# Attention with a gated feed-forward block: gates as rows through DRAM, transposes by DMA, layer normalizing on ScalarE, and a new instruction order

## The chip, the cores and the metric

One core of one Trainium2 chip. The metric is the time on the device in microseconds (us), as the median of several executions; a kernel's executions mostly agree within a few tenths of a per cent (three of the four of the kernel before took 253.68 to 254.1 us). A run counts as slow when it lies over 1.5% above the fastest run of the same kernel, and only fast runs enter the ratios. TensorE (PE in the profile) multiplies matrices, PEld is its weight load, VectorE (DVE), ScalarE (ACT) and GpSimd (POOL) do the rest, and SyncE (SP) issues transfers (DMA). The program gives each engine its own list of instructions, in a fixed order; where an input is not there yet, the engine waits (in the changed kernel VectorE stood 3.89 us for one transfer, with two normalizings behind it that did not need it).

## The reference

```python
def reference(A_x, A_wqkv, A_wo, B_x, B_w1, B_w3, B_w2, c, w_mod):
    # sizes: x (1, 2048, 512), wqkv (512, 1536), w1, w3 (512, 1792), w2 (1792, 512), w_mod (512, 3072), bfloat16
    def _A_ref(x, wqkv, wo):
        H, W, dil = 32, 8, 2                  # 32 heads of 16; a query sees 8 keys, 2 apart
        # ... cut: q, k, v; gather of 8 keys and values per query; softmax over the 8
        return (...).reshape(B, S, D) @ wo
    def _B_ref(x, w1, w3, w2):
        return (_silu(x @ w1) * (x @ w3)) @ w2          # written with einsum
    x = A_x
    mod = (_silu(c) @ w_mod).reshape(c.shape[0], 6, 1, -1)
    # ... cut: sa, ca, ga, sb, cb, gb are the six rows of mod
    h = _layernorm(x, axis=-1) * (1 + ca) + sa          # LN1
    x = x + ga * _A_ref(h, A_wqkv, A_wo)                # first gate
    h = _layernorm(x, axis=-1) * (1 + cb) + sb          # LN2
    x = x + gb * _B_ref(h, B_w1, B_w3, B_w2)            # second gate
    return x
```

The 2048 rows are handled as 16 tiles of 128.

## The kernel before

The gates are not applied to the activations: the weights `wo` and `w2` are scaled by them once. For that a gate has to lie in all 128 partitions, which four products with a stationary matrix of equal columns (`csb`) give directly. The attention weights of a tile go to DRAM (`a_scratch_dram`) and come back in another layout (`sb_al`), because there the 8 window positions lie in partitions.

```python
# Every instruction is recorded with its cost in a small model; the model plays the engines
# and so fixes, once, the order of each engine's instructions.
    def dma(self, out, in_, key, nbytes, r=(), w=(), part=(), after=(), eng="sp", cost=450, group=None):
        nc = self.nc

        def fn(e):
            a = out() if callable(out) else out
            b = in_() if callable(in_) else in_
            with nc.allow_non_contiguous_dma(reason="layout"):
                return e.dma_start(a, b)

        o = self.op(eng, fn, cost, key, r=r, w=w, part=part, after=after, dma=nbytes)
        if group is not None:
            group.append(o)
            o.group = group
        return o

    def schedule(self, prio):
        # ... cut: picks, engine by engine, the ready operation of highest priority
                if o.dma:
                    dma_free = max(busy[e], dma_free) + o.bytes // DMA_RATE
                    o.end = dma_free + LAT["sp"]
                else:
                    o.end = busy[e] + LAT[e]
        # ... cut

    def gate(i):
        k = ("mod", 4 + i)
        vm = Val("ps_gate", psum)

        def mm(e):
            for t in range(KT):
                ins = e.matmul(bank(vm), csb[:, t, :], wm_g[i][:, t, :], start=(t == 0), stop=(t == KT - 1))
            return ins

        p.op("pe", mm, 4 * MM, k, r=[vwmg[i], vcsb] + wm_hold, w=[vm])
        dst = (ga_bc, gb_bc)[i]
        p.op("act", lambda e: e.activation(dst[:], bank(vm), ACT.Copy), c_act(512), k, r=[vm], w=[vg[i]])

    def ln_stats(which, T):
        i = which * NT + T
        k = ("st", i)
        vs, vm = Val("st"), Val("mv")
        o = p.op("dve", lambda e: e.bn_stats(st[:, i, :], x_sb[:, T, :]), 670, k, r=[vx[T]], w=[vs])
        p.op("dve", lambda e: e.bn_aggr(mv[:, i, :], st[:, i, :]), 190, k, r=[vs], w=[vm], lead=o)
        va, vr = Val("var"), Val("rstd")
        o = p.op("pool", lambda e: e.tensor_tensor(rs[:, i, :], mv[:, i, 1:2], cst[:, 0:1], ALU.add), 350, k, r=[vm, vcst],
                 w=[va])
        p.op("pool", lambda e: e.tensor_tensor(rs[:, i, :], rs[:, i, :], cst[:, 1:2], ALU.pow), 550, k, r=[va, vcst],
             w=[vr], lead=o)
        vn = Val("xn", xnpool)
        p.op("dve", lambda e: e.tensor_scalar(vn.at[:], x_sb[:, T, :], mv[:, i, 0:1], rs[:, i, :], op0=ALU.subtract,
                                              op1=ALU.mult), 350, ("nm", i), r=[vx[T], vr, vm], w=[vn])
        return vn

    def ln_T(which, gi, vns):
        # ... cut: for each tile 4 transposes on TensorE into PSUM (120 ns a pair in the model),
        # then per feature block one eviction that applies the modulation (ScalarE, or VectorE
        # for half of the first two LN1 groups)

    def values(T, i, ve, va):
        vad, val = Val("ad"), Val("al", alpool)
        p.dma(bass.AP(a_dram, T * P * W * H, [[W * H, 16], [16 * W * H, 8], [1, W * H]]),
              lambda: ve.at[0][:, i].rearrange("p w h -> p (w h)"), ("ad", T), 65536, r=[va, ve], w=[vad], cost=400)
        p.dma(lambda: val.at[:], bass.AP(a_dram, T * P * W * H, [[H, P], [16 * W * H, 8], [1, H]]), ("al", T), 65536 * 3,
              r=[vad], w=[val], cost=400)
        vv = Val("vsh", vshpool)
        loads = []
        for g in range(0, 8, VG):
            p.dma(lambda g=g: vv.at[:, g:g + VG, :].rearrange("p g d -> p (g d)"),
                  bass.AP(v_dram, (PAD + T * P + g) * D, [[8 * D, 16], [-DIL * D, W], [1, VG * D]]), ("vl", T), VG * 131072,
                  r=[vv_dram[T]] + ([vv_dram[T - 1]] if T else [vvpad]), part=[vv], group=loads)

        # ... cut: one VectorE product of 128x4096 elements (value rows times attention weights),
        # 32 small products that add up the window (TensorE), then the output projection, which
        # reads `wo` already scaled by the first gate

    # ... cut; the order in which the program is recorded:
    gate(0)
    p.op("dve", lambda e: e.tensor_tensor(wo[:], wo[:], bass.AP(ga_bc, 0, [[D, P], [0, KT], [1, D]]), ALU.mult), 1200,
         ("mod", 6), r=[vwo, vg[0]], w=[vsc_wo])
    modulation(1)
    gate(1)
    # ... cut: the same for w2 in two halves, then attention in 8 blocks, then 5 FFN groups
```

The softmax here doesn't subtract the row's maximum and nothing guards it: scores larger than these inputs give would overflow.

## Time and profile before

| | before |
|---|---|
| median of 3 runs | 254.03 us (253.68 to 254.1) |
| span of the profiled run | 253.2 us |
| TensorE busy | 239.0 us (94%) |
| VectorE busy | 191.7 us (76%), over 90% from 20 to 175 us |
| first large product | 10.51 us |

The lines behind this stand in the prediction.

### The profile page before, as it was taken

To read this page: it belongs to the slowest core of one execution; us is meant where nothing else is said; L and a number is where in the kernel's file an instruction comes from. 1 tells how busy PE (TensorE), PEld (TensorE's weight loads), DVE (VectorE), ACT (ScalarE), POOL (GpSimd) and SP (SyncE) were. 2 spreads that over 40 slices of the span, in tenths; PEclk is the share of its full clock that TensorE was granted. 3 is DMA by queue.
4 is the path that set the end of the run, shared out by engine and by line. 5 is a ranking of instruction groups with operands and counts; after the bars stand their busy time and mean duration, and the time that the engine had idled before them with its cause. 6 is when DMAs were issued, how large, how long until landed. Compare 5 with 4: busy or idle time off the path is not lost.

```text
span 253.2 us, 5473 instructions
## 1 busy us (share of the span) xinstructions
PE 239.0 (94%) x2262; PEld 140.4 (55%) x2296; DVE 191.7 (76%) x298; ACT 111.4 (44%) x198; POOL 32.0 (13%) x81
## 2 busy tenths in 40 slices
PE   0599989999999999999999999999999999999995
PEld 0367555655488666546654544556544444565562
DVE  4759889999998989999899899999952443432432
ACT  2159748864863347432462273334234322420120
POOL 6237641001000040000002200020030000000000
PEclk9999999999999999999999999999999999999999
DMA  6997999899954595322369145393001000000101
GB/s 193 359 324 189 293 350 331 210 331 284 241 123 140 142 310 196 64 31 62 106 194 295 54 104 85 87 310 103 4 0 44 0 0 21 21 3 21 41 23 41
DMA packets 45817, 36.29 MB, mean 143 GB/s; under 512 B 19408, under 2 KB 36576, under 8 KB 45792
## 3 DMA queue, kind: packets, MB, share of 16 engines
q1 hardware_dynamic: 45264, 35.94, 49.4%
q8 instruction: 18, 0.29, 0.5%
q10 hardware_dynamic: 528, 0.00, 0.1%
q14 instruction: 7, 0.06, 0.1%
HBM read 30.67 MB, written 5.26 MB: 142 GB/s over the span
## 4 chain that ended last, share of the span: by engine, by line
PE 87%; DVE 5%; DMA 2%; POOL 2%; issue 1%; SPq 0%; ACT 0%; DVEq 0%
PE pall L771 36%; PE pall L792 19%; PE pall L615 9%; PE pall L755 5%; PE pall L742 5%; PE pall L633 5%; PE pall L673 4%; PE pall L574 2%; DMA sb_x<-in_A_x_dram 2%; POOL sb_rs L555 1%; DVE sb_xn L558 1%; DVE sb_st L550 1%; POOL sb_rs L553 1%; DVE sb_pq L664 1%; DVE sb_hh L780 1%
## 5 line engine op out<-in xcount | busy, mean ns | idle before, releaser
L771 PE MATMUL pall<-sb_h,sb_w 128*128 128x512 bf16 (+1 forms) x548 | 100.0, 336 | 0.7
L771 PEld LDWEIGHTS pall<-sb_h,sb_w 128*128 128x128 bf16 x560 | 53.7, 97 | 41.4
L777 ACT ACTIVATE sb_sg<-pall 128x512 bf16<-128x512 f32 (+1 forms) x70 | 35.6, 511 | 70.6 <-PE pall L771 70.3
L780 DVE TENSOR_TENSOR sb_hh<-sb_sg,pall 128x512 bf16<-128x512 bf16 (+1 forms) x70 | 39.5, 577 | 26.0 <-PE pall L771 23.8
L792 PE MATMUL pall<-sb_w,sb_hh 128*128 128x512 bf16 x216 | 49.7, 379 | 0.4
L664 DVE TENSOR_TENSOR sb_pq<-sb_q,sb_kT 128x4096 bf16<-128x4096 bf16 x16 | 36.4, 2283 | 0.5 <-ACT sb_q L622 0.3
L792 PEld LDWEIGHTS pall<-sb_w,sb_hh 128*128 128x128 bf16 x224 | 21.4, 98 | 23.5 <-DVE sb_hh L780 0.2
L615 PE MATMUL pall<-sb_h,sb_wqkv 128*128 128x512 bf16 (+1 forms) x155 | 31.9, 344 | 0.3
L582 ACT ACTIVATE sb_h<-pall,sb_modc 128x512 bf16<-128x512 bf16 (+1 forms) x36 | 23.1, 708 | 18.7 <-PE pall L574 13.1
L553 POOL TENSOR_TENSOR sb_rs<-sb_mv,sb_cst 128x1 f32<-128x1 f32 x32 | 8.8, 276 | 151.4 <-DVE sb_mv L551 148.4
L733 DVE TENSOR_TENSOR sb_vsh<-sb_vsh,sb_al 128x4096 bf16<-128x4096 bf16 x12 | 27.3, 2285 | 0.4 <-DMA sb_vsh<-v_scratch_dram 0.4
L798 DVE TENSOR_TENSOR sb_o<-pall,sb_x 128x512 bf16<-128x512 f32 x16 | 11.0, 688 | 18.0 <-PE pall L792 18.0
L550 DVE BATCH_NORM_STATS2 sb_st<-sb_x 128x6 f32<-128x512 bf16 x32 | 21.8, 682 | 3.3 <-DMA sb_x<-in_A_x_dram 3.2
L555 POOL TENSOR_TENSOR sb_rs<-sb_rs,sb_cst 128x1 f32<-128x1 f32 x32 | 20.9, 654 | 2.5
L615 PEld LDWEIGHTS pall<-sb_h,sb_wqkv 128*128 128x128 bf16 x160 | 15.1, 101 | 11.0 <-ACT sb_h L582 0.7
L633 PE MATMUL pall<-sb_wqkv,sb_h 128*128 128x512 bf16 x63 | 17.6, 411 | 1.5 <-DVE sb_xn L558 1.3
L574 PE MATMUL pall<-sb_ident,sb_xn 128*128 128x128 bf16 x128 | 12.8, 227 | 6.4 <-DVE sb_xn L558 6.4
L673 PEld LDWEIGHTS pall<-sb_E,sb_pq 128*128 128x128 bf16 x512 | 14.7, 96 | 2.7 <-DVE sb_pq L664 0.6
L748 ACT ACTIVATE sb_ot<-pall 128x512 bf16<-128x512 f32 x16 | 9.6, 598 | 13.6 <-PE pall L742 13.6
L574 PEld LDWEIGHTS pall<-sb_ident,sb_xn 128*128 128x128 bf16 x128 | 9.5, 101 | 10.6 <-DVE sb_xn L558 6.9
L755 PE MATMUL pall<-sb_wo,sb_ot 128*128 128x512 bf16 x58 | 15.0, 379 | 0.3
L673 PE MATMUL pall<-sb_E,sb_pq 128*128 128x32 bf16 x512 | 15.1, 177 | 0.0
(59 smaller groups left out, 163.8 us busy)
## 6 DMA issues: line engine op xcount, KB each, us to landing
sb_vsh<-v_scratch_dram SPq DMA_DIRECT2D x48, 256.0 KB, 4.4
sb_vshx<-v_scratch_dram SPq DMA_DIRECT2D x16, 256.0 KB, 4.5
sb_wm_s<-in_w_mod_dram SPq DMA_DIRECT2D x2, 1024.0 KB, 6.6
v_scratch_dram<-sb_v SPq DMA_DIRECT2D x16, 128.0 KB, 5.0
sb_w<-in_B_w_dram SPq DMA_DIRECT2D x4, 512.0 KB, 7.9
out_dram<-sb_o SPq DMA_DIRECT2D x16, 128.0 KB, 1.7
sb_w<-in_B_w_dram SPq DMA_DIRECT2D x1, 1792.0 KB, 8.9
sb_wqkv<-in_A_wqkv_dram SPq DMA_DIRECT2D x3, 512.0 KB, 7.9
```

Of the source, the lines that this page charges most:

```text
L550: o = p.op("dve", lambda e: e.bn_stats(st[:, i, :], x_sb[:, T, :]), 670, k, r=[vx[T]], w=[vs])
L574: ins = e.transpose(b[:, col:col + P], vns[tt].at[:, ft * P:(ft + 1) * P], ident[:])
L615: ins = e.matmul(bank(vp)[:, 0:n], wqkv[:, t, col:col + P], vh.at[:, t, 0:n], start=(t == 0), stop=(t == KT - 1))
L633: ins = e.matmul(bank(vp), vh.at[:, t, tt * P:(tt + 1) * P], wqkv[:, t, 2 * D:3 * D], start=(t == 0), stop=(t == KT - 1))
L664: return e.tensor_tensor(vp.at[:], in0, in1, ALU.mult)
L673: ins = e.matmul(b[:, c0:c0 + H], vp.at[:, w, ft, :], E_sb[:, ft, :], start=(ft == 0), stop=(ft == KT - 1))
L733: return e.tensor_tensor(v_w, v_w, a_w, ALU.mult)
L755: ins = e.matmul(bank(vy), vt.at[:, ft, :], wo[:, ft, :], start=(ft == 0), stop=(ft == KT - 1))
L771: ins = e.matmul(bank(vp)[:, 0:n], wt[:, t, fi * P:(fi + 1) * P], vh.at[:, t, 0:n], start=(t == 0), stop=(t == KT - 1))
L777: p.op("act", lambda e: e.activation(vt.at[:, 0:n], bank(vgp)[:, 0:n], ACT.Silu), c_act(n), k, r=[vgp], w=[vt], table="silu")
L780: p.op("dve", lambda e: e.tensor_tensor(vh_.at[:, 0:n], vt.at[:, 0:n], bank(vup)[:, 0:n], ALU.mult), c_dve(n), k, r=[vt, vup], w=[vh_])
L792: ins = e.matmul(bank(vz), vhh[fi].at[:, tt * P:(tt + 1) * P], w2[:, fi, :], start=(fi == 0), stop=(fi == NF - 1))
```

## The change

Its intent: take work off TensorE and VectorE and close TensorE's gaps. (1) Idle products come before the first real ones, so that those no longer run at half pace (422 ns for 512 columns at 10.5 us in the kernel before, against 216 later). (2) `c` is loaded as four rows and transposed, the first loads are merged. (3) A gate is computed as columns, transposed to rows, written to DRAM and spread over the partitions by two GpSimd DMAs. (4) LN2 is normalized on ScalarE, with a bias made by two small GpSimd steps, and for FFN groups 1 to 4 transposed by DMA. (5) The attention weights' trip is issued by GpSimd. (6) The last two tiles are computed and stored in halves. A pair of LN1 evictions of the second group goes from VectorE to ScalarE. (7) All priorities, and so the order of every engine, are new; the scheduling model now also treats GpSimd's DMAs differently. The core of the diff (cut: sizes and aliases of buffers, the calls of (1), the code of (2) and (6), the LN1 eviction, a constraint on the order of the FFN products, the priorities):

```diff
@@ -208,8 +208,11 @@
                     o.cost += TABLE_LOAD
                 busy[e] = o.start + o.cost
                 if o.dma:
-                    dma_free = max(busy[e], dma_free) + o.bytes // DMA_RATE
-                    o.end = dma_free + LAT["sp"]
+                    if e == "sp":
+                        dma_free = max(busy[e], dma_free) + o.bytes // DMA_RATE
+                        o.end = dma_free + LAT["sp"]
+                    else:
+                        o.end = busy[e] + 2 * o.bytes // DMA_RATE + LAT["sp"]
                 else:
                     o.end = busy[e] + LAT[e]
                 heapq.heappush(done, (o.end, o.n, o))
@@ -523,25 +530,48 @@
                                    stop=(t == KT - 1))
             return ins
 
-        p.op("pe", mm, 1000, k, r=[vwms[i], vcs] + wm_hold, w=[vm])
+        o = p.op("pe", mm, 1000, k, r=[vwms[i], vcs] + wm_hold, w=[vm])
         vb16 = Val("modb")
         p.op("dve", lambda e: e.tensor_copy(modc_bf[:, jlo:jlo + 8], bank(vm)[:, 0:8]), 180, k, r=[vm], w=[vb16])
         p.op("dve", lambda e: e.tensor_scalar(modc_bf[:, jlo + 4:jlo + 8], modc_bf[:, jlo + 4:jlo + 8], 1.0, None,
                                               op0=ALU.add), 180, k, w=[vb16])
         p.op("dve", lambda e: e.tensor_copy(modc[:, jlo:jlo + 8], modc_bf[:, jlo:jlo + 8]), 180, k, r=[vb16], w=[vmod[i]])
+        return o
+
+    def warm(i, after=()):
+
+        vw = Val("ps_warm", psum)
+
+        def mm(e):
+            for _ in range(4):
+                ins = e.matmul(bank(vw)[:, 0:P], ones[:], ones[:], start=True, stop=True)
+            return ins
+
+        p.op("pe", mm, 428, ("warm", i), r=[vc], w=[vw], after=after)
 
     def gate(i):
+
         k = ("mod", 4 + i)
         vm = Val("ps_gate", psum)
 
         def mm(e):
-            for t in range(KT):
-                ins = e.matmul(bank(vm), csb[:, t, :], wm_g[i][:, t, :], start=(t == 0), stop=(t == KT - 1))
+            b = bank(vm)
+            for j in range(4):
+                for t in range(KT):
+                    ins = e.matmul(b[:, j:j + 1], wm_g[i][:, t, j * P:(j + 1) * P], csT_bf[:, t:t + 1], start=(t == 0),
+                                   stop=(t == KT - 1))
             return ins
 
-        p.op("pe", mm, 4 * MM, k, r=[vwmg[i], vcsb] + wm_hold, w=[vm])
+        p.op("pe", mm, 16 * 27, k, r=[vwmg[i], vcs] + wm_hold, w=[vm])
+        vgc, vgr, vgd = Val("gcol"), Val("grow", growpool), Val("gdram")
+        p.op("dve", lambda e: e.tensor_copy(gcol[:, 4 * i:4 * i + 4], bank(vm)[:, 0:4]), 180, k, r=[vm], w=[vgc])
+        vt = Val("ps_gt", psum)
+        p.op("pe", lambda e: e.transpose(bank(vt).bitcast(bf)[0:KT, 0:P], gcol[:, 4 * i:4 * i + 4], ident[:]), 120, k,
+             r=[vgc, vident], w=[vt])
+        p.op("dve", lambda e: e.tensor_copy(vgr.at[:], bank(vt).bitcast(bf)[0:KT, 0:P]), 200, k, r=[vt], w=[vgr])
+        p.dma(bass.AP(g_dram, i * D, [[P, KT], [1, P]]), lambda: vgr.at[:], k, 4096, r=[vgr], w=[vgd], eng="pool", cost=600)
         dst = (ga_bc, gb_bc)[i]
-        p.op("act", lambda e: e.activation(dst[:], bank(vm), ACT.Copy), c_act(512), k, r=[vm], w=[vg[i]])
+        p.dma(dst[:], bass.AP(g_dram, i * D, [[0, P], [1, D]]), k, 131072, r=[vgd], w=[vg[i]], eng="pool", cost=600)
 
     def ln_stats(which, T):
         i = which * NT + T
@@ -555,6 +585,13 @@
         p.op("pool", lambda e: e.tensor_tensor(rs[:, i, :], rs[:, i, :], cst[:, 1:2], ALU.pow), 550, k, r=[va, vcst],
              w=[vr], lead=o)
         vn = Val("xn", xnpool)
+        if which:
+            vb = Val("nbias")
+            p.op("pool", lambda e: e.tensor_tensor(nb[:, T, :], mv[:, i, 0:1], cst[:, 2:3], ALU.mult), 200, k, r=[vm, vcst], w=[vb])
+            p.op("pool", lambda e: e.tensor_tensor(nb[:, T, :], nb[:, T, :], rs[:, i, :], ALU.mult), 200, k, r=[vr], w=[vb])
+            p.op("act", lambda e: e.activation(vn.at[:], x_sb[:, T, :], ACT.Identity, bias=nb[:, T, :], scale=rs[:, i, :]),
+                 c_act(512) + 50, ("nm", i), r=[vx[T], vr, vb], w=[vn])
+            return vn
         p.op("dve", lambda e: e.tensor_scalar(vn.at[:], x_sb[:, T, :], mv[:, i, 0:1], rs[:, i, :], op0=ALU.subtract,
                                               op1=ALU.mult), 350, ("nm", i), r=[vx[T], vr, vm], w=[vn])
         return vn
@@ -562,6 +599,20 @@
     def ln_T(which, gi, vns):
         vh = Val("h", hpool)
         n = len(vns)
+        if which and gi >= DMA_T:
+            k = ("tr", 2 * gi + (2 * len(LN1) if which else 0))
+            vt = Val("hT")
+            for tt in range(n):
+                p.dma(lambda tt=tt: vh.at[:, :, tt * P:(tt + 1) * P], lambda tt=tt: vns[tt].at[:], k, 157000, r=[vns[tt]],
+                      part=[vt, vh], cost=1250, transpose=True)
+            for ft in range(KT):
+                def mod(e, ft=ft):
+                    return e.activation(vh.at[:, ft, 0:n * P], vh.at[:, ft, 0:n * P], ACT.Identity,
+                                        bias=modc[:, 8 * which + ft:8 * which + ft + 1],
+                                        scale=modc[:, 8 * which + 4 + ft:8 * which + 5 + ft])
+
+                p.op("act", mod, c_act(n * P), (k[0], k[1] + 1), r=[vt, vmod[which]], part=[vh])
+            return vh
         for half in range(2):
             k = ("tr", (2 * gi + half) + (2 * len(LN1) if which else 0))
             vt = Val("ps_tr", psum)
@@ -717,9 +768,9 @@
 
         vad, val = Val("ad"), Val("al", alpool)
         p.dma(bass.AP(a_dram, T * P * W * H, [[W * H, 16], [16 * W * H, 8], [1, W * H]]),
-              lambda: ve.at[0][:, i].rearrange("p w h -> p (w h)"), ("ad", T), 65536, r=[va, ve], w=[vad], cost=400)
+              lambda: ve.at[0][:, i].rearrange("p w h -> p (w h)"), ("ad", T), 65536, r=[va, ve], w=[vad], cost=600, eng="pool")
         p.dma(lambda: val.at[:], bass.AP(a_dram, T * P * W * H, [[H, P], [16 * W * H, 8], [1, H]]), ("al", T), 65536 * 3,
-              r=[vad], w=[val], cost=400)
+              r=[vad], w=[val], cost=900, eng="pool")
         vv = Val("vsh", vshpool)
         loads = []
         for g in range(0, 8, VG):
```

## The prediction

> **What bounds the kernel now.** I read the page's totals first, then the chain that ended last, then TensorE's waits, then its timeline, then the stretches of the start. Totals and chain of the page:
>
> ```profile
> PE 239.0 (94%) x2262; PEld 140.4 (55%) x2296; DVE 191.7 (76%) x298; ACT 111.4 (44%) x198; POOL 32.0 (13%) x81
> ...
> PE 87%; DVE 5%; DMA 2%; POOL 2%; issue 1%; SPq 0%; ACT 0%; DVEq 0%
> ```
>
> TensorE is busy for 94% and makes up 87% of the chain. Busy alone proves little where ends are modelled, so I ask for what TensorE waited:
>
> ```profile
> PE pall L574 <- DVE sb_xn L558: 6.4, 2, 5.6
> PE pall L522 <- DMA sb_wm_s<-in_w_mod_dram: 1.5, 1, 1.5
> PE pall L633 <- DVE sb_xn L558: 1.3, 1, 1.3
> ```
>
> Of 6.4 us, 5.6 lie before TensorE's first instruction; 1.5 and 1.3 are also before 10.51 us. In the remaining 240 us only 1 us is left: the other 0.8 of the first line (at 36.8 us) and 0.2 for ScalarE. So the middle is a dense TensorE, in an order fixed when the program was built. Its timeline:
>
> ```profile
> 5.62 0.61 PE L574 MATMUL pall<-sb_ident,sb_xn 128*128 128x128 bf16 x4 [5.62 <-DVE sb_xn L558]
> 7.76 0.99 PE L522 MATMUL pall<-sb_csT_bf,sb_wm_s 128*128 128x1 bf16 x32 [1.54 <-DMA sb_wm_s<-in_w_mod_dram]
> ...
> 10.51 3.59 PE L633 MATMUL pall<-sb_wqkv,sb_h 128*128 128x512 bf16 x8 [1.30 <-DVE sb_xn L558]
> 13.89 1.06 PE L615 MATMUL pall<-sb_h,sb_wqkv 128*128 128x256 bf16 x4
> 14.74 0.42 PE L574 MATMUL pall<-sb_ident,sb_xn 128*128 128x128 bf16 x2
> ...
> 192.36 17.43 PE L771 MATMUL pall<-sb_h,sb_w 128*128 128x512 bf16 x79
> 209.63 1.67 PE L792 MATMUL pall<-sb_w,sb_hh 128*128 128x512 bf16 x7
> ```
>
> From start to start, 8 products of 512 columns took 13.89 - 10.51 = 3.38 us (422 ns each) at 10.5 us, while at 192 us 80 (79 recorded) took 17.27 us (216 ns). The same instruction runs at half pace until about 16 us. The page's granted clock stays at full all the while, so that row doesn't show this. Normal pace by the same subtraction: 216 ns for 512 columns, 109 for 256, 56 for 128, about 25 for 32, 16 or 1.
>
> I check the density: from 10.51 to 250.3 us the code asks for 792 products of 512 columns (171.1 us), 288 of 256 (31.4), 120 transposes (6.7), 1024 of 32 or 16 (25.4), and the second modulation (0.8): 235.4 us in 239.8. Of the 4.4 us over, 2.8 are the half-pace start: from 10.51 to 17.46 us it does 8 of 512, 20 of 256 and 4 transposes, 1.73 + 2.18 + 0.22 = 4.13 us at full pace, in 6.95. About 1.6 us are scattered. VectorE is above 90% busy from 20 to 175 us, but its waits are not in TensorE's list.
>
> [...] 422 and 216 ns, cold for some 5.5 us after 10.51.
>
> [...] This trace shows 56 ns as TensorE's pace and no DMA transpose at all.
>
> [...]
>
> ```profile
> 26.35 0.55 POOL L555 TENSOR_TENSOR sb_rs<-sb_rs,sb_cst 128x1 f32<-128x1 f32 x1
> ...
> 27.39 2.70 POOL L555 TENSOR_TENSOR sb_rs<-sb_rs,sb_cst 128x1 f32<-128x1 f32 x1
> ```
>
> The second runs beside a 2.29 us product of VectorE. [...]
>
> [...] The attention weights' round trip through SP now lands in 2.5 us each way (page part 6); GpSimd's is unmeasured.
>
> **The change, part by part.**
>
> 1. Idle products. Fourteen groups of four 128-column products before the first modulation and six after it. Cold: 14 x 4 x 0.107 = 6.0 us (half pace from the 422 ns row, divided by 4), from about 1.1 us, in time when TensorE only waits. So the clock should be free before 10 us and the 2.8 us go. But a faster TensorE meets its data: the start's stretches show the DMA engines full (shares 0.99 to 1.13 from 4 to 20 us), and the three loads of the qkv weights, issued at 3.21, 4.95 and 5.67, with landings of 6.6, 7.9 and 8.7 us, land near 9.8, 12.9 and 14.4. Warm, the eight v-products end at 10.3 + 1.73 = 12.0, ahead of the second at 12.9. I take 0.6 to 0.9 us back: gain 2.1.
>
> 2. c in rows. 528 tiny packets on the ScalarE queue go (0.1% of 16 engines' span, 0.25 us), and merging two x loads saves an SP issue of 0.43 us ahead of the modulation weights, whose landing released TensorE at 7.76. The matrix itself (1 MB) stays. First large product perhaps 0.3 us earlier. The added transpose and VectorE copy end near 5 us, before those weights land.
>
> 3. Gates. Each goes from 4 x 216 = 0.86 us to 16 x 25 = 0.40 plus one transpose of 0.06: 0.4 saved, twice, 0.8. The way through DRAM costs two GpSimd DMAs, about 5 us by the 2.5 us above. The first gate was at 18.3 us and its use (the output projection) at 59 us; the second at 63 and its use (the second FFN product) at 85. Both hidden if the order keeps such gaps.
>
> 4. LN2 transposes by DMA. FFN groups 1 to 4 hold 14 tiles with 4 transposes each: 56 x 56 ns = 3.1 us leave TensorE. The normalizing (0.41 us x 16 = 6.6 us) leaves VectorE for ScalarE, as does a pair of LN1 evictions (0.7). ScalarE gains 16 x about 0.65 = 10 us and reaches about 49%, not a bound. The path to h gets longer: two more GpSimd steps of some 0.25[...]. That is on the end only where TensorE has no FFN product of an earlier group left.
>
> 5. Attention weights from GpSimd. 32 DMAs leave SP, whose queue waited in order for other things. They cost TensorE nothing directly, but they sit in GpSimd's order beside the power for each LN, and each read waits for its write to land.
>
> 6. Tail. Now from the last product at 250.3: VectorE 0.69, issue, landing, end at 253.2. With the last two tiles in halves of 256 columns the eviction is nearer 0.42 and the store half as large: 0.3. The doubled weight loads hide; 28 x 109 = 3.05 against 14 x 216 = 3.02 us a tile, 0.06 back.
>
> Sum: 2.1 + 0.3 + 0.8 + 3.1 + 0.3 - 0.1 = 6.5 us, thus 247.5. The new order could remove part of the 1.6 us of scattered gaps, or add as much with the longer paths. I choose no net for it.
>
> **The rivals.**
>
> (a) The longer, partly serialized paths make TensorE wait in its fixed order: DMA transposes behind bulk loads on SP, or GpSimd stuck in a wait or behind VectorE's products. For it: the 2.70 us row and a like one at 34.28 us, after which TensorE stood 0.8 us at 36.8, and VectorE's density. Against: weights and v-rows come well ahead in this trace (`values` waited for a DMA 0.4 us in all), and there is FFN work to fill from 70 us on. One stall per FFN group of 1 us would give 251; several of 2 us eat the whole gain: 254 to 256.
>
> (b) The start is bound by DMA: the weights land when they land, warm or not. For: shares around 1.1. Against: 2.8 us of half-pace products sit fully in the chain. If only 1 us comes of it, 248.7.
>
> (c) VectorE is the hidden bound between 20 and 175 us, so that TensorE's 3.1 us of transposes only turn into waiting there. For: over 90%. Against: VectorE loses 7 us itself, and after 180 us it is at half load, while TensorE stays dense to the end; work is conserved on TensorE. Then still 248 or so.
>
> (d) The order is better than I allow and fills the scattered gaps: 246.
>
> **Range and chances.** Predicted 247.5. Faster by over 2% means below about 249.0, which needs 5 of the 6.5 us. The two certain terms (transposes, gates) are 3.9 and the tail 0.3; so it takes about a third of the warm-up, with no new stall. Rivals (a) and (b) each take it out of that with perhaps one chance in six. I give faster 0.68, same 0.28, slower 0.04, and 244.5 to 251.0 as the range.
>
> **What would show it.** Right: the first 512-column products at 216 ns from start to start; no half pace after 10 us; 72 LN transposes on TensorE in place of 128; gate products with one column; TensorE's waits after 10 us below 3 us; last product near 244. Wrong: a wait of TensorE for ScalarE's h or for a DMA-transposed h of more than 1 us; GpSimd DMA issues stretched beside VectorE's products; attention weights landing later than 6 us after issue; a wait for the q or k weights near 12 us beyond 0.9 us; or idle products that delay LN1's transposes.

That idle products free the clock was my estimate, from the half pace that the trace shows for some 5.5 us after 10.51. Their 0.107 us each is about a quarter of the 422 ns (0.106), and the changed kernel's first 40 then started 107 ns apart, the later ones 56. The 0.65 us of a normalizing on ScalarE is an estimate a little above the 0.60 of its 512-column evictions in the kernel before (0.81 was measured), and the 0.42 of the tail is a 128x256 product of VectorE there (419 ns).

## More of the kernel before

One view more is needed for comparison, the stretch from 40 to 50 us: its length, then for each of PE, PEld, DVE, ACT and POOL the busy us (with the number of instructions), then the granted clock of TensorE, the mean share of the 16 DMA engines that is busy, and GB/s.

```profile
40.00:50.00 10.00, 9.89 (x117) 5.67 (x116) 9.69 (x17) 8.30 (x15) 0.74 (x2) 1.00 0.96 271
```

TensorE and VectorE both have almost no gap (9.89 and 9.69 of the 10 us busy), while the DMA engines are nearly full (0.96) with the loads of the later weights.

## The result, and the profile after

| | before | after |
|---|---|---|
| median | 254.06 us (4 runs, 253.68 to 255.59) | 271.96 us (4 runs, 269.14 to 274.73, the last one slow) |
| span of the profiled run, mean granted clock | 253.2 us, 1.000 | 267.4 us, 0.981 |

The ratio of the fast runs is 1.0655, 95% interval [1.0557, 1.0753]: the changed kernel is slower by 6.5%. A ratio here is always the mean time of one kernel's fast runs over that of the other's of the same rounds, so not quite the ratio of the medians that are quoted.

The page of the changed kernel, its totals, the row of the granted clock in 40 slices of 6.7 us, and the chain that ended last:

```profile
PE 244.2 (91%) x2339; PEld 146.6 (55%) x2375; DVE 186.9 (70%) x283; ACT 122.8 (46%) x214; POOL 75.0 (28%) x149
...
PEclk9999997999799999979999999999999999999999
...
PE 50%; DMA 19%; DVE 12%; POOL 9%; issue 4%; SPq 3%; ACT 3%; DVEq 0%
```

TensorE was 87% of the chain and is now 50%; transfers hold 19% and GpSimd 9%. Nothing became a bound by its amount of work: VectorE is less busy than before, and GpSimd only 28%. What grew is waiting. The clock row drops in three slices, at about 40, 67 and 113 us. TensorE's waits (us in total, times, longest):

```profile
PE pall L625 <- DVE sb_xn L595: 4.7, 2, 3.7
PE pall L822 <- ACT sb_h L610: 3.3, 1, 3.3
PE pall L793 <- DVE sb_gcol L567: 1.6, 1, 1.6
PE pall L625 <- ACT sb_xn L592: 1.5, 1, 1.5
```

Comparing from start to start with the paces of the prediction, the places where TensorE loses most are 39.6 to 47 us (5.5 us), 61 to 68 (2.9), 72 to 75 (1.7), 94 (1.1) and 110 to 118 (4.7), some 16 us in all; the rest is mostly before 30 us, much as in the kernel before. Each of the first and the last is one wait of over 3 us, after which products run at up to twice their time until the clock is back (the granted clock was 0.50 from 43.3 to 45.75 us, 0.65 from 113.8 to 116.1 and 0.52 from there to 118); after the wait of 1.6 us that ends at 64.9 four products of 512 columns took 1.71 us, double too (clock 0.50 from 66.8 to 69.4), and after the one of 1.5 us that ends at 75.8 nothing of the kind is seen (1.00 up to 78). The stretch answering to the one above:

```profile
40.00:50.00 10.00, 6.40 (x61) 3.68 (x64) 8.22 (x11) 5.04 (x9) 1.45 (x2) 0.83 0.91 304
```

**What TensorE waits for at 39.5 us.** The chain that ended last, in order of time (start, us, what), and VectorE's timeline with the idle time before an instruction in brackets:

```profile
27.75 5.41 DMA g_scratch_dram<-sb_grow
...
33.46 8.10 DMA sb_ga_bc<-g_scratch_dram
```

```profile
41.58 1.23 DVE L885 TENSOR_TENSOR sb_wo<-sb_wo,sb_ga_bc 128x2048 bf16<-128x2048 bf16 x1 [3.89 <-DMA sb_ga_bc<-g_scratch_dram]
```

The first gate's trip through DRAM takes 13.8 us for 1 KB out and 128 KB in, with the DMA engines 97% and 100% busy in the two parts; the 128 KB stores of the output land in 1.7 us in the median. The scaling of `wo` that needs it stands in VectorE's order ahead of two normalizings of LN1, so VectorE stands still for 3.89 us, and TensorE for 3.7 us behind it, although nothing needs the scaled `wo` yet.

**What it waits for between 54 and 77 us, and at 110 us.** Again the chain, in two pieces:

```profile
54.72 7.71 DMA sb_al<-a_scratch_dram
...
62.45 2.29 DVE sb_vsh L784
...
71.47 0.60 POOL sb_gb_bc L133
...
72.74 2.14 POOL sb_nb L591
...
74.90 0.82 ACT sb_xn L592
```

```profile
102.31 2.57 POOL sb_rs L585
...
105.11 2.28 POOL sb_nb L591
...
107.41 0.82 ACT sb_xn L592
...
108.25 2.33 DMA sb_h<-sb_xn
...
110.60 2.94 ACT sb_h L610 x4
...
113.82 2.49 PE pall L822 x7
```

In the first piece a value product waits for the second trip of attention weights, which holds up the step that takes the second gate's columns out of PSUM, and LN2's bias comes after the second gate's transfer in GpSimd's queue. In the second piece LN2's chain runs from GpSimd's power to TensorE's next FFN product, 11.5 us.

A GpSimd step on 128x1 numbers lasts 0.2 to 0.4 us by itself (the power 0.55 to 0.63) and 2.1 to 2.6 us when one of VectorE's 128x4096 products runs beside it for over 2 us. In the trace of the changed kernel that holds for 8 of the 96 steps; none of the others took over 0.63 us, though some 30 lay beside shorter two-input steps of VectorE. Four of the eight are the new bias steps. LN2 now puts four such steps ahead of every tile instead of two, in a queue that also issues and awaits the trips, and ScalarE waits behind them:

```profile
ACT sb_xn L592 <- POOL sb_nb L591: 25.1, 14, 4.6
```

### The profile page after: what moved, and what is told of

It is laid out like the page before. It is cut to its first block, busy times and chain, and to the rows that moved or that the text cites. A ratio compares the mean times of both kernels' runs of the same rounds, so it can differ in the third digit from the quotient of the medians.

```text
span 267.4 us, 5690 instructions
## 1 busy us (share of the span) xinstructions
PE 244.2 (91%) x2339; PEld 146.6 (55%) x2375; DVE 186.9 (70%) x283; ACT 122.8 (46%) x214; POOL 75.0 (28%) x149
## 4 chain that ended last, share of the span: by engine, by line
PE 50%; DMA 19%; DVE 12%; POOL 9%; issue 4%; SPq 3%; ACT 3%; DVEq 0%
PE pall L822 27%; PE pall L858 12%; DMA sb_x<-in_A_x_dram 4%; PE pall L806 4%; DMA a_scratch_dram<-sb_attn 4%; SPq L133 3%; DMA sb_ga_bc<-g_scratch_dram 3%; DMA sb_al<-a_scratch_dram 3%; DVE sb_vsh L784 3%; PE pall L845 2%; POOL sb_rs L585 2%; POOL sb_rs L583 2%; DMA g_scratch_dram<-sb_grow 2%; DVE sb_st L580 2%; PE pall L793 2%
## 5 line engine op out<-in xcount | busy, mean ns | idle before, releaser
L858 PE MATMUL pall<-sb_w,sb_hh 128*128 128x512 bf16 x190 | 43.5, 379 | 0.6 <-DVE sb_hh L831 0.2
L784 DVE TENSOR_TENSOR sb_vsh<-sb_vsh,sb_al 128x4096 bf16<-128x4096 bf16 x13 | 29.7, 2288 | 4.6 <-DMA sb_vsh<-v_scratch_dram 2.7
L858 PEld LDWEIGHTS pall<-sb_w,sb_hh 128*128 128x128 bf16 x196 | 18.9, 98 | 22.1 <-DVE sb_hh L831 0.3
L583 POOL TENSOR_TENSOR sb_rs<-sb_mv,sb_cst 128x1 f32<-128x1 f32 x32 | 13.3, 416 | 58.1 <-DVE sb_mv L581 56.4
L868 DVE TENSOR_TENSOR sb_o<-pall,sb_x 128x512 bf16<-128x512 f32 (+1 forms) x18 | 11.3, 630 | 25.1 <-PE pall L858 20.0
L592 ACT ACTIVATE sb_xn<-sb_x,sb_nb,sb_rs 128x512 bf16<-128x512 bf16 x16 | 13.0, 812 | 25.1 <-POOL sb_nb L591 25.1
L133 POOL DMA_DIRECT2D sb_al<-a_scratch_dram x16 | 14.3, 899 | 25.6 <-DMA a_scratch_dram<-sb_attn 24.7
L133 POOL DMA_DIRECT2D a_scratch_dram<-sb_attn x16 | 8.7, 546 | 36.4 <-DVE sb_attn L761 36.2
L633 ACT ACTIVATE sb_h<-pall,sb_modc 128x512 bf16<-128x512 bf16 (+1 forms) x22 | 13.4, 683 | 10.0 <-DVE sb_modc L538 5.9
L684 PE MATMUL pall<-sb_wqkv,sb_h 128*128 128x512 bf16 x59 | 15.4, 392 | 1.7 <-DMA sb_wqkv<-in_A_wqkv_dram 1.3
```

The source lines that it names most:

```text
L133: return e.dma_start(a, b, transpose=True) if transpose else e.dma_start(a, b)
L784: return e.tensor_tensor(v_w, v_w, a_w, ALU.mult)
L858: ins = e.matmul(bank(vz), vhh[fi].at[:, tt * P:(tt + 1) * P], w2[:, fi, :], start=(fi == 0), stop=(fi == NF - 1))
```

## The experiments

My theory after reading the traces was: no engine has too much to do; the trips and the longer LN2 path have become latencies that the order of the instructions leaves no room for. Rivals were: GpSimd's way of issuing DMAs is itself slow; the bulk loads are the sole cause; the DMA transposes; and, later, that the parts cost their time in any order.

In all kernels the order of every engine's instructions is written out and replayed, so that an edit changes only what it says (the replayed original has the same order, waits and buffers as the original). All gave correct results. The kernels of a batch shared a chip and the runs of the kernel before; its median there was 254.98 in the first batch, 255.65 in the second, 255.53 in the third and 254.6 in the fourth.

| run | base | edit | median us | ratio to before, 95% interval |
|---|---|---|---|---|
| gates_direct | after | gates by the old broadcast product | 265.3 | 1.0393 [1.0361, 1.0424] |
| trips_on_sync | after | GpSimd's DMAs issued by SyncE | 270.77 | 1.0617 [1.0586, 1.0648] |
| ln2_old | after | LN2 wholly the old way | 264.59 | 1.0376 [1.0336, 1.0415] |
| loads_held | after | 7 bulk loads later | 271.05 | 1.061 [1.0571, 1.0649] |
| gates_ln2_old | after | both gates_direct and ln2_old | 263.64 | 1.0331 [1.0281, 1.038] |
| norm_old | after | LN2 normalized on VectorE, DMA transposes kept | 260.87 | 1.0223 [1.0175, 1.0271] |
| before_warm | before | idle products added | 254.84 | 0.9974 [0.995, 0.9998] |
| before_best | before | idle products, some DMA transposes, halved tail | 254.53 | 0.9953 [0.9927, 0.9979] |
| norm_gates | after | norm_old and gates_direct | 260.77 | 1.0231 [1.0188, 1.0273] |
| norm_gates_held | after | norm_gates and loads_held | 260.38 | 1.0198 [1.0161, 1.0235] |
| norm_gates_held_tail | after | the last, only one tile in halves | 261.66 | 1.0171 [1.0092, 1.0249] |
| nb_on_act | after | two small LN2 steps on ScalarE | 266.02 | none |
| parts_old_order | before's order | nearly the parts of norm_gates | 254.12 | 0.9987 [0.9956, 1.0018] |
| parts_gates_old_order | before's order | the same with gates through DRAM | 256.88 | 1.0091 [1.0053, 1.0129] |
| warm_dmat | before | before_best without the halved tail | 254.2 | 0.9991 [0.9961, 1.0021] |

### gates_direct: the gates without DRAM

```diff
-                    ins = e.matmul(b[:, j:j + 1], wm_g[i][:, t, j * P:(j + 1) * P], csT_bf[:, t:t + 1], ...)
+                ins = e.matmul(bank(vm), csb[:, t, :], wm_g[i][:, t, :], start=(t == 0), stop=(t == KT - 1))
-        p.dma(bass.AP(g_dram, ...), ..., eng="pool")
-        p.dma(dst[:], bass.AP(g_dram, ...), ..., eng="pool")
+        p.op("dve", lambda e: e.tensor_copy(dst[:], bank(vm)), c_dve(512), k, r=[vm], w=[vg[i]])
```

> The changed kernel with its order of instructions on every engine held fixed; only the two gates go back to the broadcast product (4 products of 512 columns), evicted by VectorE straight into the broadcast tile, so the way through DRAM is gone. Theory (late transfers in a fixed order): in the changed kernel VectorE stood 3.9 us for the gate's broadcast at 37.7 to 41.6 us and TensorE lost about 5.6 us there with the slow clock after it. Without the trip that wait is gone; but the next transfer that VectorE's order waits for, the attention weights of the second tile, lands at about 47, so part comes back: 3 to 6 us faster than the changed kernel (some 266 to 269 us by the host's clock against 272). Rival (the gate's trip was hidden, the loss is elsewhere): within 1 us of the changed kernel, 271 to 273.

Measured: 265.3 us, 6.7 less than after. TensorE's longest wait is now (the one for ScalarE's h, 3.4 us, is still there too):

```profile
PE pall L811 <- DVE sb_vsh L802: 4.8, 3, 4.2
```

The wait for the gate is gone, but a new one of 4.2 us stands in nearly the same place: VectorE's first product with attention weights, `sb_vsh`, starts at 47.47 us, against 47.81 in the changed kernel. The attention weights' trip ends at the same time with or without the gate. The first sum over the window starts on TensorE at 49.8 us instead of 50.7, so only 0.9 us is gained there; another 3.3 us or so is gained between 50 and 96 us, where the second gate's trip no longer stands among LN2's steps in GpSimd's queue. Together they are about the difference of the two profiled runs (267.4 and 263.7 us); the 6.7 us is that of the medians, and after's own runs spread over 5.6 us.

### trips_on_sync: another issuer

```diff
-eng="pool"   # on the 36 DMAs of attention weights and gates
+eng="sp"     # the same places in the order
```

> The changed kernel, order held; the 36 transfers issued from GpSimd (gates and attention weights) are issued from SyncE's queue instead, at the place that the order gives them. Theory (they are slow because 16 DMA engines are full of bulk loads until 60 us): the first ones still take 5 to 8 us to land, and SyncE, which now stands for them too, holds back other loads, so 270 to 280 us. Rival (GpSimd's software path is what is slow, or VectorE starves it): they land in 2 to 3 us even before 60 us, and the time falls by 5 us or more, to below 267.

Measured: 270.77 us, 1.2 below after, inside the spread of after's own runs (269.14 to 274.73). The chain still shows the first trips of the attention weights as slow:

```profile
39.36 5.84 DMA a_scratch_dram<-sb_attn
...
52.43 5.92 DMA a_scratch_dram<-sb_attn
58.37 7.07 DMA sb_al<-a_scratch_dram
```

After had 6.21 and 5.51 us for its first trip, and 6.36 and 7.71 for the one from 48 us. These three are as slow from SyncE. Two transfers were quick: the first read, 2.39 us, and the first gate's spread, 4.42 us against 8.10. But in their time the DMA engines were 52% and 49% busy, and in after 83% and 100%, which fits SyncE holding loads back while it waits for the trips (it issued the first read at 45.2 us, when the write had landed). So it isn't GpSimd's way of issuing; the rival falls. (parts_old_order below confirms it: it takes the kernel before's time, with the trips issued by GpSimd in place of SyncE.) The kernel's scheduling model was changed against this: it now lets GpSimd's transfers pass by the queue of SyncE's. Computed with it, the first gate's trip takes 5.8 us, against 13.8 measured; the whole kernel 249.6 us, against a span of 267.4. The old model gave 251.8 for the kernel before, against 253.2.

### ln2_old and norm_old: which half of the LN2 change

```diff
 ln2_old and norm_old:
-        if which:      # bias by two GpSimd steps, normalizing on ScalarE
-            ...
-            return vn
+        # LN2, like LN1, by VectorE's tensor_scalar
 ln2_old only:
-DMA_T = 1
+DMA_T = 5             # no group transposed by DMA
```

> The changed kernel, order held as far as it goes; the second LN is as before the change: normalized on VectorE, transposed on TensorE, evicted by ScalarE. Theory A (the longer LN2 path costs TensorE about 7 us in three waits at 74, 95 and 110 us, of which the transposes on TensorE give back 3.1): 2 to 5 us faster than the changed kernel, 267 to 270. Theory B (those waits only pass on what the late transfers before them cost): slower by 2 to 5 us, 274 to 277, as TensorE and VectorE get work back.

> The changed kernel, order held; only the normalizing of LN2 goes back from ScalarE (with two more small GpSimd steps a tile) to VectorE; its transposes stay on the DMA engines. If the loss in the LN2 path comes from GpSimd's small steps (in order behind waiting transfers, and 2.2 us when VectorE runs a product beside them), most of the 7 us that putting all of LN2 back gained comes already here: 264 to 267. If it comes from the DMA transposes and the four evictions behind them, the time stays at 270 to 273.

Measured: 264.59 and 260.87 us. Taking back the normalizing alone gives 11 us; taking back the DMA transposes as well loses 3.7 of them again (by the ratios 3.9). So within the changed order the transposes are worth about the 3.1 us that the prediction worked out, though in ln2_old I also had to choose places for the TensorE transposes, which may hold some of it. The normalizing costs 11 us. In norm_old the waits of over 1.2 us are:

```profile
PE pall L641 <- DVE sb_xn L611: 2.8, 2, 2.4
PE pall L809 <- DVE sb_vsh L800: 2.7, 3, 1.7
```

The losses of the changed kernel after 60 us are gone: the product that followed the wait at 94 us starts at 91.2 instead of 96.2, and the wait of 3.3 us at 110 doesn't occur at all.

### nb_on_act: only the two small steps moved

```diff
-            p.op("pool", lambda e: e.tensor_tensor(nb[:, T, :], mv[:, i, 0:1], cst[:, 2:3], ALU.mult), ...)
-            p.op("pool", lambda e: e.tensor_tensor(nb[:, T, :], nb[:, T, :], rs[:, i, :], ALU.mult), ...)
+            p.op("act", lambda e: e.activation(nb[:, T, :], mv[:, i, 0:1], ACT.Identity, scale=-1.0), ...)
+            p.op("act", lambda e: e.activation(nb[:, T, :], nb[:, T, :], ACT.Identity, scale=rs[:, i, :]), ...)
```

> The changed kernel, order held; only the two small bias steps of LN2 (minus mean times the reciprocal deviation) move from GpSimd to ScalarE, right before the normalizing there. Theory (GpSimd's place is the fault: its steps stand behind waits for transfers and beside VectorE's products): most of the 11 us that normalizing on VectorE gained, 261 to 265. Rival (the fault is ScalarE's place in the path, its order makes LN2 late and the SwiGLU evictions wait): 269 to 273.

Measured: 266.02 us, four runs from 260.79 to 267.56. Measured against its fastest run the others count as slow, and no ratio can be given; the median lies between what the theory and the rival expected. It points to the GpSimd steps as roughly half of the 11 us, and doesn't prove it. How the rest divides between the ScalarE pass itself and the waits in front of it stays open.

### loads_held: the bulk loads out of the way

```diff
-load.15.0 load.15.1 load.16.0 load.16.1 load.18.0 load.17.0 load.17.1   # 4.5 MB of FFN weights, at 25 to 45 us
+(the same seven, issued after the value rows of the third tile have been asked for)
```

> The changed kernel, order held on all engines but SyncE, where seven bulk loads of FFN weights (about 4.5 MB) are issued after the v rows of the third tile instead of before, so they leave the DMA engines to the small transfers from about 30 to 48 us. Theory (the trips are late because of those loads): the gate's trip shrinks from 13.8 us to below 9, the first attention weights' trips from 12 to 14 us to below 8, the waits at 40 and 62 us mostly vanish, 5 to 9 us faster: 263 to 267. Rival (the trips are slow by themselves): they stay above 11 us and the time stays at 270 to 274.

Measured: 271.05 us, no gain. The trace shows why. The first attention write is now 2.15 us long instead of 6.21 (the DMA engines 13% busy meanwhile), the whole trip 8.2 us instead of 12.0, and TensorE is busy for 19.2 of the 20 us from 30 to 50: the stall there is gone, so the load on the DMA engines did make the trip slow. But the loads came later and met the next trips:

```profile
36.64 2.15 DMA a_scratch_dram<-sb_attn
...
65.25 6.04 DMA g_scratch_dram<-sb_grow
...
72.73 0.82 ACT sb_xn L615
```

GpSimd stood in its queue until the second gate's write had landed, then made LN2's bias in 0.5 us, and TensorE had waited for it:

```profile
PE pall L648 <- ACT sb_xn L615: 5.8, 1, 5.8
```

The cost moved and did not go.

### gates_ln2_old, norm_gates, norm_gates_held, norm_gates_held_tail: do the gains add?

```diff
 gates_ln2_old          = the edits of gates_direct and ln2_old
 norm_gates             = the edits of gates_direct and norm_old
 norm_gates_held        = norm_gates, with the loads of loads_held
 norm_gates_held_tail   = norm_gates_held, with `if T >= NT - 1` for `if T >= NT - 2` (only the last tile in halves)
```

> The changed kernel's order with both the gates by the broadcast product and the second LN as before the change (each alone gave about 7 us). Theory (two separate losses, the gate's trip in VectorE's order and the LN2 path through GpSimd, ScalarE and DMA): they add up, 257 to 260 us against 272 of the changed kernel; what is left over the kernel before is the attention weights' trips in the new order, about 4 us of waits between 40 and 66 us. Rival (both heal the same wait, as one chain runs through both): little beyond one of them, 263 to 265.

> The changed kernel's order, with the gates by the broadcast product and LN2 normalized on VectorE; DMA transposes, attention weights from GpSimd, idle products and the halved end stay. Theory (two faults, the gate's trip and LN2's small steps on GpSimd): the kernel loses its excess, 255 to 258 us, level with before. Rival (the attention weights' trips from GpSimd are a third fault of their own): a wait of some 4 us at 46 to 50 us as in the run with direct gates alone, and 258 to 261.

> The same with the seven bulk loads held back until after the third tile's v rows. If the attention weights' trips are late for the loads' sake, as the run with held loads showed for the first of them (2.2 us instead of 6.4 to write), the wait at 46 to 50 us goes and nothing on GpSimd blocks LN2 any more: 252 to 255, at or below before. If holding only moves the wait later again, as in that run: no gain over the same kernel without it, 256 to 260.

> The same, with only the last tile in halves: the next to last one again in one sum of 512 columns whose first seven products need no late tile. The halved end showed a wait of 0.6 us of TensorE on the last SwiGLU tile in every run with it, none before. That wait goes: 0.4 to 0.7 us faster than the run above. Rival: the same.

Measured: 263.64 beside 264.59 for ln2_old alone; 260.77 beside 260.87 for norm_old alone. Undoing the gates gave 6.7 us by itself and nothing more once LN2's normalizing was back. The two had cured the same places: the queue of GpSimd after 50 us, and at 40 to 50 us a stall whose end is fixed by another trip. VectorE's timeline of norm_gates shows that trip:

```profile
34.54 0.42 DVE L772 TENSOR_TENSOR sb_attn<-sb_ex,sb_ssum 128x256 bf16<-128x256 f32 x1
...
48.16 2.29 DVE L795 TENSOR_TENSOR sb_vsh<-sb_vsh,sb_al 128x4096 bf16<-128x4096 bf16 x1 [5.01 <-DMA sb_al<-a_scratch_dram]
50.37 4.49 DVE L726 TENSOR_TENSOR sb_pq<-sb_q,sb_kT 128x4096 bf16<-128x4096 bf16 x2
```

From the first attention weights, ready at 34.96 us, VectorE has 8.2 us of other work (until 43.14) and the trip takes 13.2. VectorE then stands for 5.01 us, with two query-key products next in its order that start as soon as the value product is through; TensorE waits 4.7 us. Holding the loads back shortened that wait to 1.7 us, put new ones of 1.8 and 1.0 us at 72 and 85, and left the time at 260.38. The times of the tail variant (257.95 to 262.67, its profile in a slow run) decide nothing; what its trace says of the tail follows under before_best.

### before_warm: the idle products alone

```diff
+    for i in range(14):
+        warm(i)
-    modulation(0)
+    first = modulation(0)
+    for i in range(6):
+        warm(14 + i, [first])
```

> The kernel before, its order held, with the 20 groups of idle products put before, between and after the first transposes and the modulation, nothing else. Theory (the half-pace start is worth what the prediction said, 2.8 us, less what the loads give back): 251.5 to 252.5 against 254.5 before. Rival (the start is bound by the loads): 253.5 to 254.5.

Measured: 254.84, ratio 0.9974, a gain of about 0.7 us (0.05 to 1.3 by the interval). The timeline of TensorE shows what the idle products do, and the price:

```profile
10.70 1.90 PE L667 MATMUL pall<-sb_wqkv,sb_h 128*128 128x512 bf16 x8 [0.21 <-ACT sb_h L616]
13.10 0.61 PE L649 MATMUL pall<-sb_h,sb_wqkv 128*128 128x256 bf16 x4 [0.50 <-DMA sb_wqkv<-in_A_wqkv_dram]
```

Eight products of 512 columns take 1.9 us instead of 3.59, then TensorE waits for weights, 0.9 us in all. It is 1.35 us ahead at 22 us, 0.9 at VectorE's first product at 27, 0.65 from 34 to 171 us, and 0.5 at the end. VectorE last waits for an x load at 20.8 us; from there to 60 us its only gaps above 0.2 us are two of 0.71 us, at 29 and 36, in which it waits for GpSimd's power.

### before_best and warm_dmat: the parts that gain, in the old order

```diff
 both: the idle products, and
+        if which and gi >= 3:     # tiles 10 to 15: LN2 transposed by DMA
 before_best only:
+        if T >= NT - 2:           # the last two tiles in halves
```

> The kernel before, order held, with the idle products, the last two tiles in halves, and DMA transposes for the LN2 tiles of the last two FFN groups only (10 to 15), where the DMA engines are idle and the order has slack; VectorE still normalizes. Sum of the prediction's own terms: 2.1 for the clock, 0.3 for the tail, 24 transposes of 56 ns = 1.3: about 3.7 faster than before, 250.5 to 251.5. Rival (a DMA transpose cannot be hidden even there: the third group's h has about 3 us in this order): a wait at the start of the fourth FFN group of 1 to 3 us, 252 to 254.

> The kernel before in its own order with only the two parts that gained something so far: the idle products at the start and the DMA transposes of LN2 for tiles 10 to 15 (24 transposes fewer on TensorE, 1.3 us); the tail is that of the kernel before, in whole tiles. Theory (halving both last tiles made TensorE wait 0.6 us for a VectorE product at the end): 253.3 to 254.3 beside 254.5 for before_best, so ratio 0.991 to 0.995. Rival (the tail in halves costs nothing net): no better than before_best, ratio 0.995 to 0.998.

Measured: ratios 0.9953 and 0.9991; they are from different chips and their intervals overlap, so by the times the tail is undecided. The traces settle it. From the weight load of the last FFN product to the end of the span it is 9.34 us with whole tiles (before, before_warm and warm_dmat alike) and 9.75 us with halves (before_best and both kernels with parts in the old order), so the halves cost 0.4 us. In before_best TensorE waits 0.6 us for a VectorE product before the first half, which needs all 14 late SwiGLU tiles at once. In the changed order the same stretch is 9.88 us in norm_gates and norm_gates_held and 8.99 in norm_gates_held_tail, with only the last tile in halves; that is one trace. The 24 transposes that leave TensorE (1.3 us at 56 ns) gave nothing measurable over before_warm in warm_dmat. There are gains of some 0.5% at best, none of 2%.

### parts_old_order and parts_gates_old_order: the parts without the new order

At this point 5 us were left over the kernel before, and either the new order or the parts held them.

```diff
 parts_old_order: norm_gates, with
-(the changed order)
+(each engine in the order of the kernel before, new instructions put where their inputs are ready)
-DMA_T = 1
+DMA_T = 3             # tiles 10 to 15 by DMA
-                if half and not which and gi < 1:
+                if half and not which and gi < 2:      # as before
 parts_gates_old_order: the same with the gates of the change (columns, rows, DRAM, two GpSimd DMAs);
 the scaling of wo moved from about 22 to about 50 us, that of w2's first half from about 66 to 79 us
```

> The kernel norm_gates (260.8 us) has the changed order; this one has nearly the same parts (idle products, c in rows, merged first loads, attention weights written and spread by GpSimd, gates straight by the broadcast product, LN2 normalized on VectorE, DMA transposes, here for tiles 10 to 15 only, last two tiles in halves), but each engine keeps the instruction order of the kernel before, with the new instructions put where their inputs are ready. Theory (the new order is what is left of the loss: it gives the first attention weights 1.5 us of slack after their modelled return, the old order gives more than 4 us after a slower one): 253.5 to 256, that is, at the kernel before or within 1 us of it, and no wait of over 2 us for a VectorE value product between 40 and 55 us. Rival (the parts themselves, above all the attention weights' trips from GpSimd, cost the remaining 5 us in any order): 258.5 to 261.5.

> As parts_old_order, but the gates go the changed way (16 products of one column, a transpose to rows, write and spread through DRAM from GpSimd), and the scaling of the output weights, which now has to wait for it, stands at about 47 us on VectorE instead of about 20 us. Theory (a trip through DRAM is hidden where the order leaves it some 20 us, and what remains is the scaling, 1.2 us on a dense VectorE, and GpSimd steps behind the trip): parts_old_order plus 0 to 2 us, so 254 to 257.5. Rival (the gate's way costs what undoing it in the changed order gave back, whatever the order): parts_old_order plus 5 to 7 us.

Measured: 254.12 us, the kernel before within the interval; the parts cost nothing in the old order, and the new order's 6.6 us (260.77 to 254.12; 6.2 by the ratios, as the two are from different batches) are gone, which is the theory. The two kernels also differ in the DMA transposes of two groups and in one pair of LN1 evictions, which no run separates from the order. TensorE's longest wait in parts_old_order in us, after its first instruction:

```profile
PE pall L636 <- DVE sb_xn L606: 1.5, 3, 0.8
```

The trips are no faster there. Between 38 and 60 us the attention weights' writes take 4.2 to 5.5 us and their reads 5.1 to 7.1, from GpSimd, beside the same loads. VectorE has other things to do meanwhile:

```profile
38.65 0.42 DVE L772 TENSOR_TENSOR sb_attn<-sb_ex,sb_ssum 128x256 bf16<-128x256 f32 x1
...
41.64 4.49 DVE L726 TENSOR_TENSOR sb_pq<-sb_q,sb_kT 128x4096 bf16<-128x4096 bf16 x2
...
52.95 4.49 DVE L795 TENSOR_TENSOR sb_vsh<-sb_vsh,sb_al 128x4096 bf16<-128x4096 bf16 x2
```

From the first attention weights to their use VectorE has 13.9 us of work, four query-key products and two softmaxes among it, where the changed order had 8.2; the trip, 11.5 us here, fits in. And why do the parts not gain? VectorE's first and last product of this width, in the kernel before and then in parts_old_order:

```profile
27.39 2.29 DVE L664 TENSOR_TENSOR sb_pq<-sb_q,sb_kT 128x4096 bf16<-128x4096 bf16 x1 [0.34 <-ACT sb_q L622]
...
176.97 2.29 DVE L733 TENSOR_TENSOR sb_vsh<-sb_vsh,sb_al 128x4096 bf16<-128x4096 bf16 x1
```

```profile
26.73 2.26 DVE L726 TENSOR_TENSOR sb_pq<-sb_q,sb_kT 128x4096 bf16<-128x4096 bf16 x1
...
176.71 2.28 DVE L795 TENSOR_TENSOR sb_vsh<-sb_vsh,sb_al 128x4096 bf16<-128x4096 bf16 x1
```

Of a head start of 0.66 us at 27 us, 0.26 is left at 177. TensorE's own lead is 0.42 us at 33 us and 0.33 from 70 to 164: most of it is lost early, as in before_warm, and later the two kernels keep step. That VectorE sets this pace fits with its being over 90% busy there, but no run shows it, since no part kept here saves TensorE time in that stretch, and the gates' evictions were added to VectorE.

With the gates through DRAM the time is 2.8 us higher, more than the 0 to 2 that I expected (though 256.88 lies in the range of 254 to 257.5 written beside it) and less than the rival's 5 to 7. The trips themselves are hidden. What is left is VectorE's: the scaling of `wo` now stands in the dense stretch (1.16 us at 50.47), and the two halves of `w2` stand together (3.95 us at 79.49), so VectorE's products are 1.3 us late at 52 us and 2.8 late at 85. In the old order these scalings stood in places where VectorE had room.

## Why the prediction was wrong

The prediction was 247.5 us with a range to 251.0, and 0.04 for slower by over 2%; it was 271.96. Rival (a), longer paths that make TensorE wait in its fixed order, was the right one, and was sized at 254 to 256.

- **"The new order could remove part of the 1.6 us of scattered gaps, or add as much ... I choose no net for it."** This step failed first. With most of the parts kept, the order is worth 6.6 us (norm_gates against parts_old_order, with the two small differences named there). I did not look for the slack that the new priorities leave after each trip, though the scheduling model is in the source: computed by it afterwards, the first attention weights come back 1.5 us before the place where VectorE uses them, against more than 4 us in the kernel before, whose model also makes all transfers share one queue. In the traces the room was 8.2 us against 13.9, for a trip of 13.2.
- **Part 4, "two more GpSimd steps of some 0.25".** The larger loss, when undone alone: 11 us between after and norm_old. A step took 2.1 to 2.6 us beside a 128x4096 product of VectorE, as the 2.70 us row in the prediction had shown, and there were now four ahead of each tile in a queue that also waits for trips. Only 8 of some 100 steps were stretched so, and moving the two new ones to ScalarE gave back about 5.9 of the 11 us; how the 11 divide between stretched steps, the queue and ScalarE's pass stays open. I quoted that row and then sized the steps by the undisturbed duration. The other half of part 4, the transposes, was right in the changed order (3.7 against 3.1), but brought nothing measurable in the old one.
- **Part 3, "about 5 us by the 2.5 us above ... both hidden if the order keeps such gaps".** 13.8 us, since 2.5 us was the median over the whole kernel and the trip runs while the DMA engines are 96% busy (from 27 to 47 us); in the kernel before the same view had a longest landing of 7.5 us. The condition was right and was not checked: the order did not keep the gaps. Undone alone it gave 6.7 us, not in addition to part 4's.
- **Part 5, "they cost TensorE nothing directly".** Wrong through the order: 4.7 us of TensorE's time in norm_gates. Who issues the trip made little difference (transfers of 5.84, 5.92 and 7.07 us in trips_on_sync against 6.21, 6.36 and 7.71).
- **Part 1, gain 2.1.** The clock was free by 10.7 us as said, but the gain was 0.7: the loads took 0.9, and most of the rest went between 22 and 34 us, where TensorE's lead in before_warm falls from 1.35 to 0.65 us. That this is VectorE's density, rival (c), which I had set aside because "work is conserved on TensorE", is likely and not shown by a run of its own.
- **Part 2.** Not seen: the first modulation starts at 7.71 us in parts_old_order and at 7.76 in the kernel before, the first large product at 10.83 and 10.51.
- **Part 6, gain 0.3.** Wrong in sign: the halves cost 0.4 us (9.75 against 9.34 from the last FFN weight load to the end), with a wait of 0.6 us in it that the sum did not include.

What would have shown it wrong was named well: a wait for ScalarE's h of over 1 us (3.3), attention weights later than 6 us (7.7). Not borne out were the stretched GpSimd DMA issues: those of the attention weights kept to 0.53 to 0.57 and 0.89 to 0.91 us and the gates' four to 0.55 to 0.71, though 20 of the 36 ran beside a 128x4096 product of VectorE. The chances were too sure: a change of all priorities is one large unknown, and deserved more than 0.04.

Part of the loss is the clock: in the changed kernel's trace three waits are followed by products at up to twice their time and a granted clock of 0.50 to 0.65, which cost some 1.7 us after the first, 1.3 after the one that ends at 64.9 and 1.2 after the one at 110. It comes after the waits there, and no run separates the two.

## What to carry to other kernels

A trip through DRAM was hidden here where the fixed order left VectorE 13.9 us of other work for 11.5, and not where it left 8.2 for 13.2; LN2's chain of small steps, 11.5 us from GpSimd's power at 102.3 us to TensorE's product, was not hidden either. So compare the place of an issue with the place of its use, engine by engine, and with the slowest time measured under load, before counting what it saves. The gains did not add up (the gates gave 6.7 us alone, and nothing beside norm_old: 260.77 against 260.87), so undo parts in pairs as well as singly, and replay the order so that one thing changes at a time. When several engines are dense, ask which one sets the pace before crediting another with a saving.

## What the traces show of transfers and small steps

- Landing: the fastest 64 KB write of the changed kernel landed in 1.87 us, one of loads_held in 2.15 us with the DMA engines 13% busy; of the changed kernel's transfers begun between 27 and 60 us, with the engines 83 to 104% busy, those of the attention weights took 5.5 to 7.7 us and a write of 1 KB 5.4. Load is not all of it: in the kernel before, two reads issued by SyncE near 47 us landed in 2.5 and 2.7 us with the engines as full (1.08 from 46.9 to 49.6 us).
- One DMA transpose of 128x512 took 1.2 us to issue and landed in 2.3 us at least, 3.8 us in the median and 6.8 at most.
- Beside a 128x4096 product of VectorE small GpSimd steps went from 0.2 us (the power 0.55) to 2.1 to 2.6 us, while the attention weights' DMA issues stayed at 0.53 to 0.57 and 0.89 to 0.91 us. Moving the normalizing to ScalarE, behind two more such steps a tile, cost 11 us; how much of that these steps are stays open.
